# A list scheduler learns of half clock and long transfers, and orders the attention work by schedules run forwards and backwards

## The chip, the cores and the metric

The kernel runs on one core of a Trainium2 chip. The time is device time of that core in microseconds (us), from the first to the last instruction; the number for a kernel is the median of several runs. Before the change it is 806.49 us (three runs, 805.33 to 808.28).

The core's engines work side by side and meet only through semaphores: TensorE (PE in the profile; its weight loads are PEld) multiplies matrices, VectorE (DVE) and ScalarE (ACT) work on elements, GpSimd (POOL) and SyncE (SP) issue transfers here. Each engine takes its instructions strictly in the order in which the program gives them. An instruction that waits holds up all that stand behind it on its engine, ready or not. That is why an order can cost time.

## The reference

Two blocks, all in float32. First a gated linear recurrence for 4 batches, 8 heads, 768 tokens, head size 48, with a complex gate per token and channel:

```python
scale = np.minimum(mag, 0.999) / (mag + 1e-06)          # mag = |a|
for t in range(S):
    S_re, S_im = (ar * S_re - ai * S_im + kv, ar * S_im + ai * S_re)   # kv = k_t outer v_t
    y[:, :, t] = np.einsum('bhd,bhde->bhe', q[:, :, t], S_re)
```

Then its output, as 3072 tokens of 384 numbers, goes through a layer of 8 experts. Each token is sent to the one expert with the largest logit:

```python
logits = x @ w_gate
for e in range(E):
    xe = x[expert_idx == e]
    out[expert_idx == e] = gate_w[...] * (np.maximum(xe @ w1[e], 0.0) @ w2[e])
```

## The kernel before

**Stages.** The attention block fills the first half of the span, up to about 410 us. A short routing stage sorts the tokens by expert, and from about 440 us on the experts work on 31 tiles of 128 tokens. Only the attention block is touched.

**Attention without a loop over time.** Running products of the gates, P, turn the recurrence into attention: scores are (q P) against (k / P), masked to the past, then multiplied with v. The 768 tokens fall into 6 chunks of 128 (`C`), and a small state matrix per head carries the past from chunk to chunk. The 384 channels of a batch lie in 3 tiles of 128 partitions (`G`), and the 8 heads are worked on in three groups, `GROUPS`: 2, 3 and 3 heads. For every batch these functions write operations into a list:

- `load_gates(b)`: eight transfers for the gates of a batch.
- `limit(b)`: clips the gates' size. VectorE and ScalarE hand each other the data several times (`lsq`, `ls`, `ll`, `lu`, `gate`).
- `front(b)`: the running products within blocks of 16 tokens: fifteen times a product (`z`) and then a sum (`X`), each reading the one before; then the same over 8 blocks (`zc`, `carry`). All VectorE, with three copies on ScalarE.
- `fix(t)`: applies the carried products to the tile t: four products (`fx`) and two combinations, VectorE, 672 columns.
- `fold(b, t)`: forms q P (`prod`) and k / P (`kprod`) in `pk` buffers, with reciprocals through ScalarE's logarithm and exponential (`fsq`, `fs`, `fl`), and transfers that move each head's rows to its `QX` and `KX` buffers. Nine VectorE operations, nearly all of 768 columns.
- `attention(b, g)`: for a group of heads. ScalarE fills diagonal blocks in `QX` once `KX` has landed (`turn`, two instructions per head and chunk). For each chunk TensorE makes the scores of a pair of heads (`score`), VectorE masks them (`am`, "mask" in this text) and ScalarE copies out what the state needs (`kt`); TensorE makes outputs and new states (`outputs`, `turned`), and ScalarE copies them (`xf`, `st`). In the last group the finished rows are transposed (`px_ps`), copied (`xt`) and multiplied with the routing weights (`logits`).

**What sets the order.** Nothing is issued when these functions run. Each operation becomes an `Op` with an engine letter (V, A, T, S for VectorE, ScalarE, TensorE, SyncE), the time for which it holds its engine (`busy`), the time until others may use its result (`late`), the operations whose results it needs (`after`), and those that must have let go of a buffer (`free`). The functions `dve`, `act`, `pe` and `dma` set the two times from the size. `in_time(ops)` then plays the list: it keeps a clock per engine, always takes the engine that can go first, and among the operations that are ready gives precedence by `first` (0 for masks and state copies, 1 or 2 for other work that TensorE waits for, the batch and group for TensorE's own, 5 otherwise), and then by `way`, the longest path to the end of the list. The operations are emitted in the order in which they were taken, and `InOrder` keeps that order on each engine. So every engine's queue is fixed when the kernel is built. The times in the list only decide the order; on the chip the semaphores decide when an instruction runs. All these instructions are recorded by one helper (L110 in the profile), so they are told apart by their tiles.

In the list before, transfers to `QX` and `KX` are reckoned at 3.5 us until use, the gates at 6.0, a pair of diagonals at 0.24 us on ScalarE, and TensorE always at its full clock.

Of the kernel before, what the change touches and what calls it, by code (L numbers as in the profile page):

```python
# [13 lines left out]
ALU = mybir.AluOpType  # L14
# [3 lines left out]
B, H, S, D = 4, 8, 768, 48  # L18
# [10 lines left out]
RING = 6  # L29
NT = N // 128  # L30
# [17 lines left out]
class Op:  # L48
# [3 lines left out]
    def __init__(self, engine, busy, late, emit, after, free, first):  # L52
        self.engine, self.busy, self.late, self.emit, self.first = engine, busy, late, emit, first
        self.after, self.free = [o for o in after if o], [o for o in free if o]
        self.start = None

    def ready(self):
        t = 0.0
        for o in self.after:
            t = max(t, o.start + o.late)  # L60
        for o in self.free:
            t = max(t, o.start + (o.busy if o.engine == self.engine else o.late))
        return t


def in_time(ops):


    users, left, way = {}, {}, {}
    for o in ops:  # L70
        left[o] = len(o.after) + len(o.free)
        for p in o.after + o.free:
            users.setdefault(p, []).append(o)
    for o in reversed(ops):
        way[o] = o.late + max((way[u] for u in users.get(o, ())), default=0.0)
    able, clock, out = {e: [] for e in "VATS"}, dict.fromkeys("VATS", 0.0), []

    def let(o):
        able[o.engine].append((o.ready(), o))
    for o in ops:  # L80
        if not left[o]:
            let(o)
    while len(out) < len(ops):
        best = None
        for e, l in able.items():
            if l:
                t = max(clock[e], min(x[0] for x in l))
                if best is None or t < best[0]:
                    best = t, e
        t, e = best  # L90
        r, o = min((x for x in able[e] if x[0] <= t), key=lambda x: (x[1].first, -way[x[1]]))
        able[e].remove((r, o))
        o.start, clock[e] = t, t + o.busy
        out.append(o)
        for u in users.get(o, ()):
            left[u] -= 1
            if not left[u]:
                let(u)
    return out
# [14 lines left out]
def gateloop_then_moe(ctx, tc, q, k, a_re, a_im, v, wg, w1, w2, out):  # L114
# [61 lines left out]
    with ExitStack() as att:  # L176
# [11 lines left out]
        def buf(nm, *shape):  # L188
            return one.tile([128, *shape], FP32, name=nm)
# [13 lines left out]
        zs = [buf(f"z{i}", 2, 2, NC) for i in range(2)]  # L203
# [3 lines left out]
        fx = [buf(f"fx{i}", BL * C * (NB - 1)) for i in range(4)]  # L207
        fs, fl = buf("fs", BL, C * NB), buf("fl", BL, C * NB)
# [6 lines left out]
        xts = [buf(f"xt{i}", DT, 128) for i in range(2)]  # L215
# [31 lines left out]

        heads, seq = {}, [0]
        state = {}

        def load_gates(b):
            for i in range(BL // JQ):
                js = slice(i * JQ, i * JQ + JQ)
                old = state.get(("gate", i), [])
                state["raw", i] = [dma(6.0, lambda p=p, src=src, i=i, js=js: Q.dma_start(gates[i][:, :, p, :], src[b, :, js, :]),
                                       free=old) for p, src in ((1, a_re), (2, a_im))]
# [26 lines left out]
        def front(b):  # L283

            o = None
            for j in range(1, BL):
                g, r = gates[j // JQ], j % JQ
                w, readers = ring("z", 2)
                z = zs[w]
                prev = dims(g[:, r - 1], 2 * NC, (-NC, 2), (0, 2), (1, NC)) if j == 1 else dims(X[:, j - 1], NC, (-NC, 2), (0, 2), (1, NC))  # L290
                m = dve(4 * NC, lambda z=z, g=g, r=r, prev=prev: vtt(z, dims(g[:, r], 0, (NC, 2), (NC, 2), (1, NC)), prev, ALU.mult),
                        state["scaled", j // JQ] + [o], readers)
                if j == 1:
                    c0 = act(2 * NC, lambda g=g: A.copy(X[:, 0], g[:, 0, 1:3, :]), state["scaled", 0], state.get("X", []))
                o = dve(2 * NC, lambda z=z, j=j: vtt(X[:, j], z[:, 0], z[:, 1], ALU.add), [m], state.get("X", []))
                taken_by(readers, o)
                state["gate", j // JQ] = [m, c0] if j < JQ else [m]

            end = X[:, BL - 1]
            l1 = act(2 * NC, lambda: A.copy(last[:, 1:3, :], end), [o], state.get("last", []))  # L300
            l2 = act(NC, lambda: A.activation(last[:, 0, :], end[:, 1], func=ACT.Copy, scale=-1.0), [o], state.get("last", []))
            o = dve(36, lambda: V.tensor_copy(carry[:, :, :, 1], end.rearrange("p u (n b) -> p u n b", b=NB)[:, :, :, 0]), [o],
                    state.get("carry", []))
            for n in range(2, NB):
                w = n % 2
                m = dve(4 * G * C, lambda n=n, w=w: vtt(zc[w], dims(last, n - 1, (NC, 2), (NC, 2), (NB, G * C)),
                                                        dims(carry, NC + n - 1, (-NC, 2), (0, 2), (NB, G * C)), ALU.mult), [o, l1, l2])
                o = dve(2 * G * C, lambda n=n, w=w: vtt(carry[:, :, :, n], zc[w][:, 0], zc[w][:, 1], ALU.add), [m])
            state["last"] = [m]
            state["carried"] = [o, c0]  # L310
            state["X"], state["carry"] = [], []

        TC = C * NB

        def fix(t):
            ts = slice(t * TC, t * TC + TC)
            xv = X[:, :, :, ts].rearrange("p j u (n b) -> p j u n b", b=NB)[:, :, :, :, 1:]
            shape = [128, BL, C, NB - 1]
            part = {}
            f = [x.rearrange("p (j n b) -> p j n b", j=BL, b=NB - 1) for x in fx]  # L320
            for i, (x, w) in enumerate(((0, 0), (1, 1), (0, 1), (1, 0))):
                part[i] = dve(672, lambda i=i, x=x, w=w: vtt(f[i], xv[:, :, x], bc(carry[:, w:w + 1, t * C:t * C + C, 1:], shape), ALU.mult),
                              state["carried"], state.get(("fx", i), []))
            state["carry"] += part.values()
            re = dve(672, lambda: vtt(xv[:, :, 0], f[0], f[1], ALU.subtract), [part[0], part[1]], [part[2]])
            im = dve(672, lambda: vtt(xv[:, :, 1], f[2], f[3], ALU.add), [part[2], part[3]])
            for i in range(4):
                state["fx", i] = [(re, re, im, im)[i]]
            return [re, im]

        def fold(b, t, fixed):
# [3 lines left out]
            sq = act(1536, lambda: A.activation(fsq, X[:, :, :, ts], func=ACT.Square), fixed + state["carried"], state.get("fsq", []))  # L335
# [11 lines left out]
                        fixed + state["carried"] + [lq], rq) for u in range(2)]  # L347
# [7 lines left out]
            for u in range(2):  # L355
                def ev(u=u):
                    e = kp[:, u, S:KW].rearrange("p (c w) -> p c w", w=2)
                    A.copy(e[:, :, u], end[:, :, 0])
                    A.activation(e[:, :, 1 - u], end[:, :, 1], func=ACT.Copy, scale=(-1.0, 1.0)[u])
                evs.append(act(12, ev, fixed + state["carried"], rk, n=2))  # L360
# [7 lines left out]
            state["X"] += [sq, *prod, *evs, *kprod]  # L368
            taken_by(rq)
            taken_by(rk)  # L370
            for h, p0, n, d0 in segments(t):
# [6 lines left out]
                for u in range(2):  # L378
                    to = slice(u * D + d0, u * D + d0 + n)
                    qd.append(dma(3.5, lambda u=u, p0=p0, n=n, to=to, slot=slot: Q.dma_start(  # L380
                        QXs[slot][to, :, 0:128], qp[p0:p0 + n, u, 0:S].rearrange("p (c t) -> p c t", c=C)), [prod[u]], old))
                    kd.append(dma(3.5, lambda u=u, p0=p0, n=n, to=to, slot=slot: Q.dma_start(
# [6 lines left out]
        def attention(b, g):  # L389
# [15 lines left out]
            for c in range(C - 1):  # L405
                for i in range(n):
# [4 lines left out]
                    turn[c, i] = act(96, diagonal, kd[i], state.get(("head", slots[i]), []), first=2, n=2)  # L411
            st, evict = None, None
            y_old = state.setdefault("y", [None])
            for c in range(C):
# [71 lines left out]
                if g == G - 1:  # L486
# [6 lines left out]
                    wx, xt_readers = ring("xt", 2)  # L493
                    xt = act(DM, lambda wx=wx: A.copy(xts[wx], px_ps), [px], xt_readers, first=1)
                    state["px"] = [xt]

                    def logits(c=c, wx=wx):
                        for d in range(DT):
                            T.matmul(lg_ps[:, c, :], lhsT=xts[wx][:, d, :], rhs=wgate[:, d * E:d * E + E], start=(d == 0), stop=(d == DT - 1))
                    lg = pe(3, logits, [xt], state.get("lg", []), first=rank)  # L500
                    taken_by(xt_readers, lg)
                    r0 = b * S + c * 128
                    away = dma(3.5, lambda c=c, r0=r0: Q.dma_start(x_hbm[r0:r0 + 128, 0:DM].rearrange("(n j) w -> j n w", j=BL), xf[:, c, :]), rows)
# [9 lines left out]
        for b in range(B):  # L513
            front(b)
            if b + 1 < B:
                load_gates(b + 1)
# [4 lines left out]
            if b + 1 < B:  # L521
                limit(b + 1)
# [303 lines left out]
```

## Time and profile before

| stretch (us) | what | TensorE busy | VectorE busy | ScalarE busy | TensorE clock |
|---|---|---|---|---|---|
| 20 to 80 | first batch's gates and products | 0 of 60 | 59.4 | 32.4 | 1.00 |
| 80 to 340 | four batches, overlapped | 195.2 of 260 | 227.6 | 180.2 | 0.50 to 1.00 |
| 340 to 400 | attention of the last batch | 53.5 of 60 | 26.3 | 38.5 | 0.82 to 1.00 |
| 400 to 460 | end of attention, routing | 28.2 of 60 | 18.9 | 5.6 | 0.50 to 0.76 |
| 460 to 780 | experts | 311.5 of 320 | 49.8 | 16.7 | 1.00 |

The rows are added up from the profile's table of stretches of 20 us. The span of the profiled run is 804.7 us. The last attention operation, a copy of the routing logits, runs at 409.54 us.

How to read the lines that follow. A row of the timeline gives the start, the time taken, the engine, the operation and its tiles (written <- read), and in brackets the idle time of the engine before it with what ended the wait. A row of the waits gives who waited for whom: us in total, how often, the longest. When VectorE is idle before `am`, the mask at the head of its queue is waiting for scores, and everything behind it waits too. In a table of stretches each engine has its busy time and, in brackets, its number of instructions; the granted clock is 1.00 when TensorE runs at full speed.

Of the transfers that feed the scores (`KX<-pk` and `QX<-pk`, 48 of about 145 KB each), the profile gives a median of 3.7 us from issue to landing, and of the gates 3.1 and 3.5 us.

### The profile page before, as it was taken

How to read it: one execution, taken by the hardware profiler on the slowest of the kernel's cores; microseconds unless marked ns; L12 is line 12 of the kernel's file. 1: busy time of each engine (PE TensorE's matmuls, PEld its weight loads, DVE VectorE, ACT ScalarE, POOL GpSimd, SP SyncE). 2: the span in 40 equal slices, each digit the busy share in tenths (PEclk: the TensorE clock that was granted, in tenths of full speed). 3: DMA queues.
4: the chain of work that ended last, by engine and by line, in shares of the span. 5: the costliest groups of instructions: out<-in, count | busy, mean ns of one | idle time of the engine just before them, and what ended most of it. 6: DMA issues, size and time to landing. Idle time of an engine off the chain costs nothing. (4 is left out here: it accounts for less than half of the span.)

```text
span 804.7 us, 11063 instructions
## 1 busy us (share of the span) xinstructions
PE 607.4 (75%) x3985; PEld 522.1 (65%) x3985; DVE 393.3 (49%) x720; ACT 284.4 (35%) x870; POOL 138.1 (17%) x160
## 2 busy tenths in 40 slices
PE   0000689818992789789931999999999999999997
PEld 0000589718992679679930877777778777777775
DVE  4999789988899778954135011111110111111110
ACT  4654588747884684587420000000000000000000
POOL 7000000000000000000012223333333333333310
PEclk9999999859995799889965899999999999999999
DMA  7222673366453651563113887879887898789840
GB/s 216 59 59 52 152 181 99 108 150 158 125 142 103 144 127 51 147 160 80 41 23 92 348 334 285 312 290 391 309 292 302 341 386 295 293 336 332 309 153 1
DMA packets 67629, 156.49 MB, mean 194 GB/s; under 512 B 9873, under 2 KB 50866, under 8 KB 59634
## 3 DMA queue, kind: packets, MB, share of 16 engines
q0 software_dynamic: 12896, 108.36, 35.1%
q1 hardware_dynamic: 51474, 47.36, 22.9%
q8 instruction: 33, 0.54, 0.3%
q10 hardware_dynamic: 3200, 0.01, 0.2%
q14 instruction: 26, 0.21, 0.1%
HBM read 127.23 MB, written 10.83 MB: 172 GB/s over the span
## 5 line engine op out<-in xcount | busy, mean ns | idle before, releaser
L110 PE MATMUL bank<-QX,KX 128*128 128x224 f32 (+1 forms) x384 | 90.5, 378 | 135.4 <-DVE fl L110 88.0
L773 PEld LDWEIGHTS h_ps<-xt,w1t 128*128 128x128 f32 x1488 | 173.7, 194 | 13.0 <-issue 5.1
L773 PE MATMUL h_ps<-xt,w1t 128*128 128x128 f32 x1488 | 174.0, 278 | 4.7 <-issue 4.7
L779 PE MATMUL o_ps<-w2t,ht 128*128 128x384 f32 x496 | 167.8, 492 | 8.3 <-ACT ht L775 8.2
L110 PEld LDWEIGHTS bank<-QX,KX 128*128 128x128 f32 x384 | 72.1, 212 | 142.3 <-issue 88.8
L775 ACT ACTIVATE ht<-h_ps 128x512 f32<-128x512 f32 x31 | 18.5, 597 | 357.7 <-PE h_ps L773 357.7
L779 PEld LDWEIGHTS o_ps<-w2t,ht 128*128 128x128 f32 x496 | 91.7, 190 | 71.5 <-ACT ht L775 14.0
L110 PE MATMUL bank<-st,QX 128*128 128x128 f32 x576 | 107.1, 276 | 1.5 <-ACT st L110 1.5
L781 DVE TENSOR_SCALAR yo<-o_ps,xs 128x384 f32<-128x384 f32 x31 | 19.1, 618 | 143.9 <-PE o_ps L779 143.9
L110 PEld LDWEIGHTS bank<-st,QX 128*128 128x128 f32 x576 | 86.2, 192 | 2.2 <-ACT st L110 1.9
L768 DVE COPY xt<-xt_ps 128x384 f32<-128x384 f32 x31 | 17.3, 557 | 140.3 <-PE xt_ps L766 140.3
L110 ACT ACTIVATE QX<-diag,KX 96x48 f32<-96x48 f32 x320 | 77.1, 327 | 19.0 <-DMA KX<-pk 19.0
L110 PE MATMUL bank<-vb,am 128*128 128x128 f32 x384 | 72.7, 279 | 7.1 <-ACT xf L110 7.0
L110 DVE TENSOR_TENSOR am<-bank,causal 128x256 f32<-128x256 f32 (+1 forms) x120 | 42.5, 367 | 62.3 <-PE bank L110 56.5
L543 POOL MEMSET state<- 128x1152 f32 x1 | 1.1, 1063 | 390.6 <-PE bank L110 390.6
L782 POOL DMA_INDIRECT out_dram<-yo,idx x31 | 31.5, 1016 | 194.9 <-DVE yo L781 194.0
L110 PEld LDWEIGHTS bank<-vb,am 128*128 128x128 f32 x384 | 58.2, 192 | 9.8 <-ACT xf L110 9.6
L110 PE MATMUL bank<-vb,kt 128*128 128x128 f32 x320 | 59.2, 278 | 0.0
L110 PEld LDWEIGHTS bank<-vb,kt 128*128 128x128 f32 x320 | 48.0, 195 | 0.1
L110 DVE TENSOR_TENSOR z<-gate,X 128x576 f32<-128x576 f32 x56 | 42.2, 754 | 1.0
L110 DVE TENSOR_TENSOR fx<-X,carry 128x672 f32<-128x672 f32 x48 | 38.8, 853 | 0.1
L110 ACT COPY st<-bank 128x384 f32<-128x384 f32 (+1 forms) x60 | 26.5, 442 | 28.6 <-PE bank L110 28.2
(143 smaller groups left out, 662.6 us busy)
## 6 DMA issues: line engine op xcount, KB each, us to landing
KX<-pk SPq DMA_DIRECT2D x48, 146.2 KB, 3.7
QX<-pk SPq DMA_DIRECT2D x48, 144.0 KB, 3.7
gate<-in_a_re_dram SPq DMA_DIRECT2D x16, 288.0 KB, 3.1
gate<-in_a_im_dram SPq DMA_DIRECT2D x16, 288.0 KB, 3.5
kt_in<-in_k_dram SPq DMA_DIRECT2D x12, 384.0 KB, 4.4
qt<-in_q_dram SPq DMA_DIRECT2D x12, 384.0 KB, 3.8
vb<-in_v_dram SPq DMA_DIRECT2D x24, 192.0 KB, 3.0
x_hbm<-xf SPq DMA_DIRECT2D x24, 192.0 KB, 2.9
```

The lines of the kernel that those rows point to most:

```text
L110: return lambda *a, **kw: self.tc.keep_in_program_order(f(*a, **kw))
L543: nc.gpsimd.memset(state, 0.0)
L768: nc.vector.tensor_copy(xt, xt_ps)
L773: nc.tensor.matmul(h_ps[:, f, :], lhsT=w1t[:, c:c + 128], rhs=xt[:, d, :], start=(d == 0), stop=(d == DT - 1))
L775: nc.scalar.activation(ht[:, 0:FT // 2, :], h_ps[:, 0:FT // 2, :], func=ACT.Relu)
L779: nc.tensor.matmul(o_ps, lhsT=ht[:, f, :], rhs=w2t[:, f * DM:f * DM + DM], start=(f == 0), stop=(f == FT - 1))
L781: nc.vector.tensor_scalar_mul(y, o_ps, xs[:, DM:W])
L782: nc.gpsimd.indirect_dma_start(out=out[:, :], out_offset=bass.IndirectOffsetOnAxis(ap=idx[:, j:j + 1], axis=0), in_=y, in_offset=None, bou ...
```

## The change

The list's costs and its search are changed; the operations themselves are not, apart from one buffer.

- **Costs.** TensorE's operations count twice for 5.5 us (`SLOW`) after it has been idle for more than 3 us (`REST`). Transfers into `QX` and `KX` and of finished rows count 5.0 us instead of 3.5, gates 7.5 instead of 6.0, a pair of diagonals 0.448 us instead of 0.24.
- **Search.** `turns` plays the list under any order of precedence, in either direction. `in_time` plays it forwards with the old precedence, then backwards from the end with the operations that finished last going first, then forwards again with the precedence that the backward play gives, and so on: four forward plays. It keeps the one whose modelled end is earliest and emits by start time. The fixed classes of `first` thus only shape the first play.
- **Finer dependencies.** `front` can work on some tiles alone, and the waits on `X`, `carry` and `last` are kept per tile; it is still called with all three tiles, `front(b, range(G))`. `load_gates(b + 1)` is written into the list after the batch's attention.
- **Memory.** One `xt` buffer instead of two; the `z` buffers are allocated later.

The core of the diff:

```diff
+REST, SLOW = 3.0, 5.5
...
+    def lag(self, user):
+        return self.busy if user.engine == self.engine and self not in user.after else self.late
...
-        r, o = min((x for x in able[e] if x[0] <= t), key=lambda x: (x[1].first, -way[x[1]]))
...
+    key = {o: (o.first, -way[o]) for o in ops}
+    best = None
+    for _ in range(4):
+        start, slow, twice = {}, [0.0], set()
+
+        def begin(o, t, idle):
+            start[o] = t
+            if o.engine == "T":
+
+                if t > idle + REST:
+                    slow[0] = t + SLOW
+                if t < slow[0]:
+                    twice.add(o)
+            return t + o.busy * (1 + (o in twice))
+        turns(ops, needs, users, lambda o: max((start[p] + p.lag(o) + (p.busy if p in twice else 0.0) for p in needs[o]), default=0.0),
+              key, begin)
+        end = max(start[o] + o.late for o in ops)
+        if best is None or end < best[0]:
+            best = end, sorted(ops, key=lambda o: start[o]), start
+
+        back = {}
+
+        def begin_back(o, t, _):
+            back[o] = t
+            return t + o.busy
+        turns(ops, users, needs, lambda o: max((back[u] + u.busy + o.lag(u) - o.busy for u in users[o]), default=0.0),
+              {o: -start[o] - o.busy for o in ops}, begin_back)
+        key = {o: -back[o] - o.busy for o in ops}
+    return best[1]
...
-        xts = [buf(f"xt{i}", DT, 128) for i in range(2)]
+        xt = buf("xt", DT, 128)
...
-                state["raw", i] = [dma(6.0, lambda p=p, src=src, i=i, js=js: Q.dma_start(gates[i][:, :, p, :], src[b, :, js, :]),
+                state["raw", i] = [dma(7.5, lambda p=p, src=src, i=i, js=js: Q.dma_start(gates[i][:, :, p, :], src[b, :, js, :]),
...
-                    qd.append(dma(3.5, lambda u=u, p0=p0, n=n, to=to, slot=slot: Q.dma_start(
+                    qd.append(dma(5.0, lambda u=u, p0=p0, n=n, to=to, slot=slot: Q.dma_start(
...
-                    kd.append(dma(3.5, lambda u=u, p0=p0, n=n, to=to, slot=slot: Q.dma_start(
+                    kd.append(dma(5.0, lambda u=u, p0=p0, n=n, to=to, slot=slot: Q.dma_start(
...
-                    turn[c, i] = act(96, diagonal, kd[i], state.get(("head", slots[i]), []), first=2, n=2)
+                    turn[c, i] = act(96, diagonal, kd[i], state.get(("head", slots[i]), []), first=2, n=4.6)
...
-            front(b)
-            if b + 1 < B:
-                load_gates(b + 1)
+            front(b, range(G))
...
             if b + 1 < B:
+                load_gates(b + 1)
                 limit(b + 1)
```

## The prediction

> **What bounds the kernel now.** The chain that ended last reaches back only to 778 us, inside the expert stage, so it says nothing of the attention stage. I read the stretches of 20 us first (length, then busy us of TensorE, its weight loads, VectorE, ScalarE, GpSimd, then granted TensorE clock, DMA share, GB/s).
>
> ```profile
> 140.00:160.00 20.00, 16.91 (x139) 16.48 (x137) 19.86 (x40) 15.18 (x43) 0.00 (x0) 0.90 0.41 115
> 160.00:180.00 20.00, 2.65 (x7) 1.89 (x7) 17.67 (x24) 8.83 (x26) 0.00 (x0) 0.50 0.60 136
> 240.00:260.00 20.00, 6.31 (x42) 5.85 (x40) 19.93 (x29) 10.28 (x24) 0.00 (x0) 0.62 0.34 92
> 380.00:400.00 20.00, 18.89 (x148) 18.70 (x148) 3.91 (x11) 9.84 (x41) 0.00 (x0) 1.00 0.15 41
> 460.00:780.00 320.00, 311.50 (x1889) 246.22 (x1888) 49.80 (x84) 16.72 (x28) 109.93 (x114) 1.00 0.82 313
> ```
>
> VectorE is full while TensorE stands still around 160 and 250, so until about 345 us VectorE sets the pace; from there to 409.7 (the copy into `lg_all`) TensorE does. The 395 us after 409.7 are routing and experts, which the diff does not touch: they stay. Next, VectorE's waits between 79 and 338 us (engine, who waits, for whom: total, times, longest):
>
> ```profile
> DVE am L110 <- PE bank L110: 20.8, 24, 3.4
> DVE am L110 <- ACT st L110: 5.3, 3, 1.8
> DVE ls L110 <- ACT lsq L110: 2.6, 2, 1.3
> DVE zc L110 <- ACT last L110: 0.8, 1, 0.8
> ```
>
> With 0.4 for a gate these are 29.9 us in which the bounding engine does nothing. Where the largest come from is in the timeline at the start of the first head group:
>
> ```profile
> 86.98 0.95 DVE L110 TENSOR_TENSOR fl<-fl,kt_in 128x768 f32<-128x768 f32 x1
> 90.50 0.43 DVE L110 TENSOR_TENSOR am<-bank,causal 128x256 f32<-128x256 f32 x1 [2.57 <-PE bank L110]
> 91.99 0.42 DVE L110 TENSOR_TENSOR am<-bank,causal 128x256 f32<-128x256 f32 x1 [1.07 <-PE bank L110]
> 93.48 0.42 DVE L110 TENSOR_TENSOR am<-bank,causal 128x256 f32<-128x256 f32 x1 [1.07 <-PE bank L110]
> 93.83 0.95 DVE L110 TENSOR_TENSOR pk<-X,qt 128x768 f32<-128x768 f32 x1
> 95.20 0.95 DVE L110 TENSOR_TENSOR pk<-X,fl 128x768 f32<-128x768 f32 x1
> ```
>
> Three masks stand in VectorE's queue ahead of products of the next group that were ready. The list put them where it expected their scores; the scores came later, 1.5 us apart. The same picture stands at 179.6 and 269.0.
>
> **What the Trainium skill says.** "TensorE: Matmul & The Clock Gate", section "What's actually happening": after an idle window of about 3.4 us TensorE runs at half rate until it has been busy for as long. The trace agrees: after the rest of 17.1 us before 177 us the granted clock is 0.58 in 180 to 184 and 1.00 in 184 to 190. "Perfetto Trace Analysis", section "DMA Instruction — HWDGE (DVE, Sync)": the row of an issue does not contain the movement of the data. It agrees: an issue of `KX<-pk` takes 0.7 us, its landing comes 3.7 us after it. "VectorE: DVE Perf Modes", section "The DRAIN you can't avoid": a semaphore between two instructions cost nothing in its test. Here it differs: a 128x576 product starts its follower after 0.67 us, but after 0.79 if that follower reads it (288 wide: 0.40 against 0.49).
>
> **The change, part by part.** No attention instruction is added or dropped: 552 VectorE operations stand in both lists. So a gain can only come from gaps. My marker is the end of the second key product (`kprod`) of group 0 of each batch, since TensorE's work on that batch can't start earlier. In the trace: 79.8, 169.2, 258.2, 337.4 us. I summed, in the order in which both built programs emit them, VectorE's instructions up to each marker, each at the start-to-start time of its kind in the trace (0.87 for 768 columns, 0.77 for 672, 0.67 for 576, 0.37 for 288, 1.27 for the gate scaling, 0.33 and 0.21 for masks): before 63.7, 140.5, 217.3, 280.1; after 61.8, 135.2, 214.1, 278.0. From marker 0 to 3 the old list holds 216.4 us of work in 257.6 us: 41.2 us lost, 29.9 of it the waits above.
>
> (a) *Waits of group-0 masks on TensorE.* Before: 5.5, 4.9 and 5.2 us in the first three batches, 15.6 together. The scores became usable 10.7, 10.5, 10.8 us after the marker (transfers, diagonals, half clock). The new list, which reckons 5.0 us for these transfers (3.5 before), 0.448 us for a pair of diagonals (0.24 before; the trace has 20 diagonals in 4.61 us, 0.46 a pair) and double time after a rest, puts 11.7, 8.9 and 11.6 us of VectorE work into that space: no wait in the first and third batch, 1.6 in the second. From the first to the last of the six masks it puts 10.8, 6.6 and 10.9 us of work; the trace needed about 10 us at half clock. So the second batch waits some 3 us more, unless TensorE is warm there, which the new list wants: it keeps the last outputs of the previous batch for that moment. Small misfits 0.6 each in the others. Left: 5.8, saved about 10 (bounds 6 and 15.6).
>
> (b) *The other waits, 14.3 us:* masks of group 1 (1.73, 1.73, 3.39, 1.79) and two squares (1.3 each) that come late from ScalarE. ScalarE was overbooked by underpriced diagonals (`ACT QX` 77.1 us busy). With a price near the trace's they should no longer pile up in front of the `st` and `lsq` work. But which waits vanish can't be read from an order. Bounds 0 and 14; I take 7.
>
> (c) *Chained front instructions.* Products and sums of the recurrence that follow each other directly: 62 such pairs from marker 0 to 3 before, 25 after, because single masks now stand between them. 37 x 0.10 = 3.7 us saved.
>
> (d) *Work moved behind marker 3:* two correction products of group 1 and two masks of batch 2, 280.1 - 278.0 = 2.1 us. Group 1's key products follow the marker by 12.9 us of work then, 12.2 before, and TensorE is busy with group 0 for longer than that, so the path doesn't wait for them.
>
> (e) *One buffer for transposed rows instead of two* (`xt`): copy and logits now alternate. A copy is 0.48 us and the hop back about 0.2, 24 copies. It lies on the path only in the last chunks, where copy and logits took turns before as well. 0 to +2; I take 0, other matmuls stand between. The gate loads issue under a reuse wait as before; behind them stand transfers of group 2, needed only after group 1's roughly 20 us on TensorE. Free. The per-tile dependencies of `front` change nothing, as it still takes all tiles in one call.
>
> (f) *The tail*, marker 3 to 409.7: 72.3 us, TensorE at 18.8 of 20. Its order is nearly the same in both programs (two score pairs and the last logits exchanged). A rest of 5.96 us before it may shrink, as outputs of batch 2 now lie there: -3 if the clock stays up; +5 if those outputs hold up the first scores. I take 0.
>
> Sum: 10 + 7 + 3.7 + 2.1 = 22.8 us. 806.5 - 22.8 = 784.
>
> **The rivals.** *Forecast*: half of the waits and part of the chaining go, 784 us. *All waits go*: 15.6 + 14 + 3.7 + 2.1 = 35, so 772. For it: the new costs match the trace. Against it: in the third cycle both engines are tied. From the first mask of group 0 to the last of group 2 there are 54 us of VectorE work plus chaining, and TensorE alone, in the last batch where VectorE was free, took 56.5 (345.9 to 402.4). *Waits come back*: single masks between recurrence instructions stop the whole recurrence if TensorE lags; (a) at its low end, (b) zero, tail +2: 806.5 - (6 + 0 + 3.7 + 2.1) + 2 = 797. For it: masks waited 3.4 us once at 293, in the middle of a front. *No net change*: the gap moves from VectorE to TensorE's tail, 806. Against it: the tail's own work fits in TensorE's queue behind the marker. *Slower*: about 18 masks a batch now stand singly in the front; if each lags by 0.5 us in three batches, 27 us are added, against 16 saved by (a), (c) and (d), with 2 for `xt`: 820. Against it: in the trace of before, single masks inside a front mostly show no wait (116.7, 120.0, 125.9 us).
>
> **How the numbers follow.** Forecast 0.60, all waits go 0.13, waits come back 0.16, no net change 0.05, slower 0.06. The time is the forecast's. The range, 772 to 801, runs from the full removal to a little beyond the return of the waits: 771 is 15.6 + 11 + 3.7 + 2.1 + 3 saved, 801 is 6 + 2 + 2 saved with 5 added in the tail. Faster by over 0.5%: 0.60 + 0.13 + 0.15 = 0.88; same 0.06, slower 0.06.
>
> **What would show it.** Markers near 78, 162, 243 and 315 us; the three waits of 2.6, 1.1, 1.1 at the first masks gone in batches 0 and 2; the VectorE total of `am` on TensorE before marker 3 down from 20.8 to about 10; 72 us from marker 3 to the end of attention; the stage after it unchanged at 395. It would be wrong if masks of groups 1 and 2 gather new waits of over half a microsecond each, if TensorE's share of the path starts well before marker 3, or if the tail grows by what VectorE saves.

## The result and the profile after

The changed kernel takes 767.98 us (four runs, 767.43 to 768.28), beside 805.91 us for the kernel before on the same chip. The ratio is 0.9525, 95% interval 0.9502 to 0.9547: 38 us faster. The direction and the place were as forecast. The size was not: 784 us was forecast with 772 as the lower end.

The stretches of 20 us after, chosen as those of before were:

```profile
120.00:140.00 20.00, 19.67 (x154) 19.07 (x153) 20.00 (x45) 16.58 (x51) 0.00 (x0) 1.00 0.38 104
140.00:160.00 20.00, 12.47 (x70) 11.60 (x68) 20.00 (x29) 10.61 (x29) 0.00 (x0) 0.70 0.62 155
220.00:240.00 20.00, 4.55 (x24) 4.27 (x24) 19.88 (x27) 9.07 (x21) 0.00 (x0) 0.58 0.53 124
340.00:360.00 20.00, 20.00 (x161) 19.86 (x160) 4.20 (x12) 12.95 (x56) 0.00 (x0) 1.00 0.11 30
420.00:740.00 320.00, 311.90 (x1892) 246.65 (x1891) 50.38 (x85) 16.72 (x28) 109.90 (x114) 1.00 0.82 315
```

VectorE (third pair) is busy for the whole of most stretches now, and TensorE still rests around 150 and 230: VectorE bounds this half as before, but without holes. The expert stretch is the same to 0.4 us. VectorE's waits between the first and the last marker of the prediction (78 to 301 us), where before had 29.9 us in five rows:

```profile
DVE am L132 <- PE bank L132: 1.8, 5, 0.8
DVE fs L132 <- ACT fsq L132: 0.9, 1, 0.9
DVE fs L132 <- ACT fl L132: 0.5, 1, 0.5
```

They are nearly all gone, of both kinds: masks that waited for TensorE, and inputs that came late from ScalarE. The timeline of VectorE at the first head group, for the place where three masks stood in the way before:

```profile
86.78 0.95 DVE L132 SCALAR_TENSOR_TENSOR fs<-fsq 128x768 f32<-128x768 f32 x1
87.65 1.82 DVE L132 TENSOR_TENSOR pk<-X,fl 128x768 f32<-128x768 f32 x2
89.39 0.16 DVE L132 TENSOR_SCALAR good<-fs 128x6 f32<-128x6 f32 x1
89.46 0.75 DVE L132 TENSOR_TENSOR am<-bank,causal 128x256 f32<-128x256 f32 x2
90.12 0.75 DVE L132 SCALAR_TENSOR_TENSOR ls<-lsq 128x576 f32<-128x576 f32 x1
90.79 0.42 DVE L132 TENSOR_TENSOR am<-bank,causal 128x256 f32<-128x256 f32 x1
91.12 1.35 DVE L132 TENSOR_TENSOR gate<-gate,ls 128x1152 f32<-128x1152 f32 x1
```

The products of the next group (`pk<-X,fl`) now stand ahead of the masks, and other ready work stands between them. No row carries a wait. The copy into `lg_all`, which ends attention, starts at 371.32 us (409.54 before):

```profile
371.32 0.20 ACT L132 COPY lg_all<-bank 128x48 f32<-128x48 f32 x1 [0.93 <-PE bank L132]
```

From there to the end of the span it is 394.9 us, 395.1 before. Of the 38.4 us between the two profiled spans, 38.2 lie ahead of this copy.

**Where it came from.** I took VectorE's instructions one by one between marker 0 and marker 3 and compared each start-to-start time with the usual one of its kind. What is above it I counted as a wait if the engine stood idle for more than 0.12 us, as chaining if the next instruction reads the result, and as other otherwise. "Group-0 waits" are those before the six masks of a batch's first head group. "Tail" is marker 3 to the copy. Two consecutive instructions normally overlap by some 0.1 us (a product of 768 columns lasts 0.95 us, and the next one starts after 0.87), and a wait loses that too. So this count gives 32.8 us of waits before, where the idle time in the view is 29.9.

| us | before | after | saved | predicted |
|---|---|---|---|---|
| waits of group-0 masks (a) | 17.1 | 1.5 | 15.6 | 10 |
| other waits (b) | 15.7 | 2.4 | 13.3 | 7 |
| chaining (c) | 7.6 | 3.2 | 4.4 | 3.7 |
| work ahead of marker 3 (d) | 280.1 | 278.0 | 2.1 | 2.1 |
| tail (f) | 72.2 | 70.1 | 2.1 | 0 |
| other | | | 0.7 | 0 |
| sum | | | 38.2 | 22.8 |

By idle time alone, the measure that the prediction used, (a) went from 15.7 to 1.3 us and (b) from 14.1 to 2.0: 14.4 and 12.1 saved. Row (d) is the sum of usual times again, over the instructions that the traces show ahead of marker 3.

### The profile page after: what moved, and what is told of

Same layout as the page of the kernel before. It is cut to its first block, busy times and chain, and to the rows that moved or that the text cites. A ratio compares the mean times of both kernels' runs of the same rounds, so it can differ in the third digit from the quotient of the medians.

```text
span 766.3 us, 11061 instructions
## 1 busy us (share of the span) xinstructions
PE 602.1 (79%) x3985; PEld 521.7 (68%) x3985; DVE 387.1 (51%) x720; ACT 280.3 (37%) x870; POOL 137.8 (18%) x160
## 5 line engine op out<-in xcount | busy, mean ns | idle before, releaser
L132 PE MATMUL bank<-QX,KX 128*128 128x224 f32 (+1 forms) x384 | 87.4, 367 | 102.6 <-DVE fl L132 86.1
L132 PEld LDWEIGHTS bank<-QX,KX 128*128 128x128 f32 x384 | 70.4, 207 | 105.0 <-issue 86.0
L132 PE MATMUL bank<-st,QX 128*128 128x128 f32 x576 | 109.9, 279 | 1.7 <-ACT st L132 1.7
L132 PEld LDWEIGHTS bank<-st,QX 128*128 128x128 f32 x576 | 87.9, 195 | 2.9 <-ACT st L132 2.9
L132 ACT ACTIVATE QX<-diag,KX 96x48 f32<-96x48 f32 x320 | 80.6, 329 | 3.8 <-DMA KX<-pk 3.7
L132 PE MATMUL bank<-vb,am 128*128 128x128 f32 x384 | 73.5, 282 | 4.9 <-DVE am L132 3.0
L132 PEld LDWEIGHTS bank<-vb,am 128*128 128x128 f32 x384 | 60.3, 196 | 6.6 <-DVE am L132 3.7
L132 DVE TENSOR_TENSOR am<-bank,causal 128x256 f32<-128x256 f32 x120 | 43.0, 363 | 33.8 <-PE bank L132 28.9
L785 POOL DMA_INDIRECT xs<-x_hbm,idx x31 | 30.2, 975 | 26.0 <-DVE idx L765 16.9
```

The lines of the kernel that those rows point to most:

```text
L132: return lambda *a, **kw: self.tc.keep_in_program_order(f(*a, **kw))
L785: nc.gpsimd.indirect_dma_start(out=o, out_offset=None, in_=src, in_offset=bass.IndirectOffsetOnAxis(ap=index, axis=0))
```

## The experiments

Each ratio is against the kernel before, run beside it on the same chip. The untouched stage behind attention differs by up to 7 us from profile to profile (394.1 to 401.3 us), so the table gives the end of attention too, from the one profile of each kernel. The two profiles of the changed kernel put that end at 371.3 and 371.2. Waits and chaining are counted as above; what each kernel is, the text below says.

| kernel | ratio, interval | attention ends | group-0 waits | other waits | chaining | tail |
|---|---|---|---|---|---|---|
| before | 1 | 409.5 | 17.1 | 15.7 | 7.6 | 72.2 |
| neither | 1.005, 1.0035 to 1.0065 | 414.0 | 15.3 | 18.0 | 7.5 | 76.1 |
| diagonals_priced_old_search | 0.9833, 0.9776 to 0.9889 | 393.9 | 11.3 | 3.6 | 9.3 | 73.5 |
| clock_and_transfers_old_search | 0.9807, 0.9784 to 0.9831 | 393.6 | 1.8 | 10.9 | 6.9 | 76.9 |
| costs_only | 0.9786, 0.9756 to 0.9816 | 396.8 | 0.9 | 14.1 | 8.4 | 75.4 |
| search_only | 0.9837, 0.9809 to 0.9865 | 396.8 | 11.6 | 14.3 | 2.5 | 72.5 |
| cheap_diagonals | 0.9725, 0.9702 to 0.9749 | 387.8 | 1.7 | 13.7 | 2.6 | 73.1 |
| diagonals_priced_search | 0.9591, 0.9534 to 0.9648 | 375.4 | 5.7 | 2.6 | 3.6 | 68.4 |
| no_half_clock | 0.9562, 0.9531 to 0.9592 | 375.1 | 4.1 | 2.6 | 3.3 | 69.6 |
| short_transfers | 0.9549, 0.9522 to 0.9577 | 371.9 | 1.8 | 1.7 | 2.7 | 70.9 |
| after | 0.9525, 0.9502 to 0.9547 | 371.3 | 1.5 | 2.4 | 3.2 | 70.1 |
| one_diagonal_done | 0.9758, 0.9701 to 0.9816 | 392.8 | 14.9 | 4.4 | 7.6 | 68.8 |

**Costs or search?** My theory was that right prices do it; the rival, that the search does. With the changed kernel, three more make all four combinations: `costs_only` has the new prices and a single play, `search_only` the old prices and four plays. `neither` puts both back. Beside the lines below, the prices 7.5 and 5.0 of the transfers become 6.0 and 3.5 there, and the diagonals' `n=4.6` becomes `n=2`:

```diff
-    for _ in range(4):
+    for _ in range(1):
...
-                if t < slow[0]:
+                if False:
```

> The changed file with the old costs and a single forward play: only one xt buffer, the later place of the gate loads in the list, the finer waits and the buffers' new places remain. Theory 'order' (the gain is all in the emitted order): within 0.5% of 806. Rival 'memory' (the buffers or the single xt did it): near 768 to 785.

> The new costs, one forward play with the old precedence. Theory 'costs' (right prices put the masks where the scores arrive; VectorE's waits of about 30 us go because of them): near 775, group-0 mask waits below 2 us a batch. Theory 'search' (the backward plays did it): 795 or more, with waits still above 20 us. If both are needed in part: 785 to 795.

> Old costs (transfers 3.5 and 6.0, diagonals 0.24, no half clock), four plays. Theory 'costs': 798 or more, since the masks stand too early again at every group 0 (about 5 us of wait a batch). Theory 'search': near 775.

Measured: `neither` is 0.5% slower than the kernel before, so the gain is in the order and not in buffers or the list's form. The two halves are worth about the same, 2.1% and 1.6% by the ratio, and attention ends at 396.8 us with either; together they are worth 4.75%. Neither theory holds in both runs: costs alone gave 794 us with 15 us of waits, where the one expected 775 and the other 795 or more with over 20 us of waits. Search alone gave 798 us, as the first had it, but is a gain all the same. What came is the third case, that both are needed in part. Costs alone clear group 0 (17.1 to 0.9 us). But the old search then leaves 14 us of other waits, now at different places:

```profile
DVE am L132 <- PE bank L132: 6.3, 5, 3.8
DVE z L132 <- ACT gate L132: 3.9, 3, 2.4
DVE ls L132 <- ACT lu L132: 2.8, 3, 1.4
```

The waits for `gate` stop the recurrence itself, and those for `lu` stop the limits that feed it. That the old precedence lets the next batch's limits come late is my reading and was not tested. Search alone more than halves the chaining (7.6 to 2.5) and leaves 26 us of waits, as it still packs masks where the false prices say that scores will be:

```profile
DVE am L132 <- PE bank L132: 19.1, 17, 2.0
DVE ls L132 <- ACT lu L132: 3.9, 2, 2.8
```

Which part of the search does its share, the backward play or dropping the fixed classes of `first`, was not tested.

**Which price?** One price at a time was put back in the changed kernel. For the half clock `if t < slow[0]` became `if False`, for the diagonals `n=4.6` became `n=2`, for the transfers 7.5 became 6.0 and 5.0 became 3.5.

> The changed kernel but the list never doubles TensorE's times. Theory 'costs': the first six masks of batches with a rest before them are placed for scores 0.8 us apart while they come 1.5 us apart: some 3 us of wait in each of three batches, 774 to 780. Theory 'search': 768 to 771.

> The changed kernel with a pair of diagonals at the old 0.24 us. If the price of the diagonals is what cleared the waits of group 1 and of the squares on ScalarE (theory 'diagonals'): VectorE's waits on ScalarE and of group-1 masks before marker 3 rise from some 2 to 8 us or more, ratio to before 0.962 or more against 0.9525. If the search cleared them whatever the price (theory 'search clears ScalarE'): 0.950 to 0.956.

> The changed kernel with the transfers at the old 3.5 and 6.0 us. Theory 'landing price': the first masks of group 0 stand about 1.5 us too early, one wait of 1 to 2 us a batch, ratio 0.956 to 0.962. Rival: 3.5 is near the measured landing of 3.7, so nothing is lost, 0.951 to 0.955.

The diagonals are the dear one: without their price the kernel takes 788 us, and 11 of its extra 16 us are waits other than group 0's:

```profile
DVE am L132 <- PE bank L132: 5.3, 8, 1.9
DVE ls L132 <- ACT lu L132: 4.1, 4, 1.8
DVE fs L132 <- ACT fsq L132: 2.0, 1, 2.0
DVE z L132 <- ACT gate L132: 1.1, 2, 0.8
```

Every row but the first names something that ScalarE delivers late. The half clock is worth 4 us of attention (375.1 against 371.3), of which 2.6 are group-0 waits; some 3 us in each of three batches had been expected, and the intervals of the two ratios overlap. For the transfers alone no loss can be told: attention ends at 371.9, and in this profile the stage that no edit touches took 401.3 us, the longest of all. The search with the diagonals' price alone, without the other two:

> Old transfers, no half clock, four plays; only the diagonals have the new price. If the diagonals' price plus the search is nearly the whole change: ratio 0.955 to 0.962. If transfers and half clock cover for each other when one is taken out (each alone cost 0.3%), more is lost together: 0.965 or more.

It gave 0.9591, in the first of the two ranges. Group-0 waits are 5.7 us there, 1.5 in the changed kernel.

**Two prices, two waits?** The same prices under the old search, to see each without the search:

> Old transfers, no half clock, one forward play with the old precedence; only the diagonals have the new price. If this price carries most of the costs' share: ratio 0.980 to 0.988, near costs_only's 0.9786. If transfers and half clock carry it when the search is plain: 0.995 or more.

> One forward play with the old precedence; half clock and long transfers priced, the diagonals at the old 0.24 us. Theory 'two prices, two waits': the waits of group-0 masks on their scores (17 us before) fall to about 5 us or less, those of group 1 and of the squares (14 us before) stay above 8; ratio 0.985 to 0.995. Rival 'the diagonals cause both': group-0 waits stay above 12 us, ratio 0.995 or more.

Each price acts mainly on its own kind of wait, though not on it alone. Against `neither`, the diagonals' price takes the other waits from 18.0 to 3.6 us and group 0 only from 15.3 to 11.3. Half clock and transfers, which were not taken apart here, take group 0 from 15.3 to 1.8 and the others only from 18.0 to 10.9. VectorE's waits from marker 0 to 3, first with the diagonals priced, then with clock and transfers:

```profile
DVE am L132 <- PE bank L132: 11.2, 10, 2.3
DVE ls L132 <- ACT lu L132: 2.2, 5, 0.6
```

```profile
DVE am L132 <- PE bank L132: 6.8, 7, 1.3
DVE fs L132 <- ACT fl L132: 3.2, 4, 1.2
```

Both ratios, 0.983 and 0.981, are within noise of the two together in a single play (0.979): a single play does not add up what its prices are worth. The second one came out lower than the 0.985 to 0.995 that I expected.

**The world made to fit the price.** Instead of raising the price I took away half of the diagonals' work in the kernel before, and left its order alone:

```diff
-            nc.gpsimd.memset(QXs[i][0:R2, :, 128 + R2:], 0.0)
+            nc.gpsimd.memset(QXs[i][0:R2, :, 128:], 0.0)
...
-                        for w in range(2):
+                        for w in range(1):
```

> The kernel before, in which ScalarE fills only one of the two diagonals of a pair (the other stays zero, so the imaginary half of the state is left out); the order is untouched. Now the old price of 0.24 us is true. Theory 'price gap' (VectorE waited because ScalarE ran later than its list said): the first mask of group 0 comes 8 to 9 us after the marker in place of 10.7, waits of VectorE before marker 3 fall from 30 to about 15 us, ratio 0.975 to 0.985. Rival 'ScalarE's lateness is hidden': 0.995 to 1.00.

The ratio is as the theory said, but the way there was not quite. The first mask of group 0 came 10.1 us after the first marker and not 8 to 9, and group 0 kept 14.9 us of waits. The others fell from 15.7 to 4.4:

```profile
DVE am L110 <- PE bank L110: 13.4, 13, 2.1
DVE am L110 <- ACT QX L110: 2.5, 3, 1.2
DVE am L110 <- ACT st L110: 0.3, 1, 0.3
```

The waits on `lsq` are gone and those on `st` nearly so. Two places in VectorE's timeline, first in the kernel before:

```profile
113.47 0.42 DVE L110 TENSOR_TENSOR am<-bank,causal 128x256 f32<-128x256 f32 x1 [1.73 <-ACT st L110]
125.24 0.76 DVE L110 SCALAR_TENSOR_TENSOR ls<-lsq 128x576 f32<-128x576 f32 x1 [1.32 <-ACT lsq L110]
```

The same two with half of the diagonals, the mask now in one row with the next one:

```profile
110.14 0.62 DVE L110 TENSOR_TENSOR am<-bank,causal 128x256 f32<-128x256 f32 x2
120.75 0.75 DVE L110 SCALAR_TENSOR_TENSOR ls<-lsq 128x576 f32<-128x576 f32 x1
```

This is the same order as before with ScalarE on time. So most of group 1's waits and those of the squares came from diagonals that ran twice as long as the list said, and group 0's did not.

**The single buffer, more plays, more slack.** Three edits around the changed kernel: two `xt` buffers again, `range(24)` for `range(4)`, `n=6.0` for `n=4.6`; then the last two together beside the changed kernel itself.

> The changed kernel with two buffers for the transposed rows, planned anew. If one buffer costs nothing, as predicted: within 0.4% of the changed kernel, ratio 0.949 to 0.956. If it costs up to the 2 us of the prediction: 0.950 or less.

> The changed kernel with 24 plays in place of 4. If the search had already settled: ratio 0.950 to 0.955. If more plays pack VectorE further: below 0.950.

> The changed kernel with a pair of diagonals at 0.56 us, above the 0.46 of the trace. If the gain comes from a price that is true: 0.954 to 0.960, a little worse on the other side. If it comes from leaving ScalarE slack: below 0.950.

> A pair of diagonals at 0.56 us and 24 plays, beside the changed kernel on the same chip. If slack for ScalarE beyond the true price is worth something: 0.3% or more faster than the changed kernel, ratio 0.949 or below. If the true price is enough: within 0.3% of it.

> The changed kernel itself, for comparison on the same chip: ratio 0.950 to 0.955, attention ending some 70 us after marker 3.

Two buffers gave 0.9524 (0.9497 to 0.955), 24 plays 0.9519 (0.9498 to 0.9541): both are the changed kernel's time. The dear diagonals gave 0.9495 (0.9442 to 0.9549), an interval that leaves both expectations open. Side by side, dear diagonals with 24 plays took 767.19 us (765.46 to 767.58) and the changed kernel 769.05 (768.18 to 769.59), ratios 0.9508 (0.9488 to 0.9528) and 0.9534 (0.9515 to 0.9553). That is 0.24%, under the 0.3% that was to count. It is more than noise, though: all five runs lie below all five of the changed kernel, and attention ends at 369.5 us against 371.2 (369.1 with the dear price and four plays). The gain lies in the tail, 67.8 us against 70.4; marker 3 comes no earlier. Whether ScalarE's slack makes it, or an order that happens to suit the tail, is open.

Where the search is plain, the buffer shows. In `neither` marker 3 is at 337.9 us, near the 337.4 of before, and its tail is some 4 us longer. TensorE's timeline at its end:

```profile
409.05 0.55 PE L132 MATMUL bank<-ident,xf 128*128 128x128 f32 x3 [0.62 <-ACT xt L132]
409.43 0.73 PE L132 MATMUL bank<-wgate,xt 128*128 128x8 f32 x6
410.79 0.55 PE L132 MATMUL bank<-ident,xf 128*128 128x128 f32 x3 [0.62 <-ACT xt L132]
411.17 0.73 PE L132 MATMUL bank<-wgate,xt 128*128 128x8 f32 x6
412.53 1.45 PE L132 MATMUL bank<-wgate,xt 128*128 128x8 f32 x6 [0.62 <-ACT xt L132]
```

Transposing, copying and logits follow each other with nothing between, and TensorE waits for the copy three times, 1.9 us of the 4. No run had two buffers under the plain search, so where the rest comes from is open. In the changed kernel most of these transposes stand between the outputs of earlier chunks; what the buffer costs then can't be seen.

## Why the prediction fell short

**What held.** VectorE was the bound (in 160 to 180 us it was busy for 17.7 of 20 us, not quite full as I had it), the gain is mostly idle time of VectorE taken away before marker 3, and the stage behind attention did not move. Marker 0 came at 77.8 us, as forecast (78). The later ones show the missing saving: 151.8, 234.6 and 301.2 us came in place of 162, 243 and 315. Step (d) was right to 0.1 us. Step (c) gave 4.4 against 3.7 us: it took 0.10 us a pair, and 36 fewer pairs saved 0.12 each (a sum of 288 columns takes 0.49 us against 0.37; the 0.40 that I set against it once was wrong).

**The step that failed is the choice of half in (b):** "I take 7" of 14.3 us. It measured 13.3 (12.1 as idle time). I held that which waits vanish can't be read from an order. But I had the cause in hand: diagonals 0.46 us a pair in the trace and 0.24 in the list. `one_diagonal_done` (15.7 to 4.4 us) and `diagonals_priced_old_search` (18.0 to 3.6) show that this one error made most of these waits, so correcting it removes them together, and not every second one. Taking half was a hedge that no row supported. The right price alone did not make it certain, though: `costs_only` has it too, and the old search left 14.1 us of other waits, now for `gate`, `lu` and scores. Clearing those took the search as well.

**The second mis-sized term is (a):** 10 us predicted, 15.6 measured, 14.4 of them idle time. The 5.8 us that I left standing came mostly from the second batch: 1.6 us at its first mask and 3 more for scores at half clock. It waited 1.5 in all. The first mask could run 9.7 us after the marker, not 10.5. Six masks then took 8.3 us, where I had set about 10 from the other batches. The warm TensorE that I had named as the one way out was not the reason: its granted clock was 0.52 in 158 to 162 us and 0.62 in the next four. What made these scores come sooner was not taken apart. The "small misfits" of 0.6 us in the other batches did not show either. In the first cycle no wait at all was left.

**(f)** was put at 0 between -3 and +5 and came out at -2.1. The rest of 5.96 us before the last batch shrank to 1.18 and 0.36, since outputs of batch 2 lie there now. The clock held, as the stretches around the first scores show, before and then after:

```profile
337.00:342.00 5.00, 0.47 (x3) 0.38 (x2) 5.00 (x8) 1.89 (x3) 0.00 (x0) 0.50 0.95 242
342.00:347.00 5.00, 3.33 (x8) 2.52 (x9) 3.18 (x5) 4.18 (x19) 0.00 (x0) 0.50 0.87 226
```

```profile
301.00:306.00 5.00, 4.32 (x36) 3.71 (x34) 5.00 (x9) 3.21 (x11) 0.00 (x0) 1.00 0.96 255
306.00:311.00 5.00, 3.54 (x13) 3.13 (x14) 5.00 (x8) 4.96 (x18) 0.00 (x0) 0.74 0.89 195
```

It is 0.50 in both stretches before and 1.00 and 0.74 after. That this is the reason for the 2 us is argued, not shown: the tail of other orders ran from 67.7 to 76.9 us. **(e)** was right for the changed kernel. Under the plain search the three waits for the buffer, 1.9 us, come to its upper bound of 2.

**The rivals.** "All waits go", 772 us, was the one that happened: (a) to (d) saved 35.4 us, its sum, with 2.1 us of tail and 0.7 of other terms on top. I gave it 0.13. What I held against it was TensorE and VectorE tied in the third cycle. The tie was there: from the first mask to the last it took 57.1 us, against the 56.5 that TensorE needs alone. It did not bind, since VectorE had other work between the masks: the cycle took 66.6 us from marker to marker, 2.7 above its work, with one wait of 0.3. The range ended at 772 because its low end counted only 11 us of (b), which gave 13.3, and because the total that it rested on, 771, was rounded up to 772.

## What to carry to other kernels

When an order made from a cost list leaves waits, compare each price in the list with the trace first; here one false price on a busy helper engine made most of a whole family of waits, and correcting it cleared the family, not a share of it. Forecast such a fix with the full family and argue for what must remain. Refining the order by plays in both directions was worth about as much again here, and each needed the other: with false prices the plays left 26 us of waits, with true ones 4, and true prices in a single play left 15.

## What the runs showed of the hardware

- The transfers that open a batch were mostly slower than the page's median tells. `KX<-pk` lands after 3.7 us in the median of all 48 before. In windows of 11 us from the first three markers the 146 KB ones took 5.4, 5.3 and 5.9 us in the median before, and 5.6, 6.2 and 6.1 after; from marker 3 it was 4.0 and 4.6. The list's 5.0 is nearer to what group 0 met than the median that I set against it.
- An operation of the running products on VectorE (128x36 to 128x576) whose follower reads its result held that follower up by 0.12 to 0.15 us: 7.6 us over 61 such pairs before, 3.2 over 25 after.
- In the changed kernel a rest of 1.9 us (157.5 to 159.45) was followed by first scores at a mean clock of 0.52 (158 to 162 us), after 0.90 in the four us before. No rest between 140 and 160 us was longer than 2.4. So TensorE was at half clock here without a rest of the 3.0 us (`REST`) from which the list counts.
- After the rest of 17.1 us in the kernel before, TensorE started at 177.14. The mean of 0.58 in 180 to 184 us and 1.00 after it put the return to full clock at about 183.4 (an estimate from these means), some 6 us after the start. That is longer than the 3.4 us with which the prediction saw agreement, and near the list's 5.5 (`SLOW`).
